# Attention and gated convolution in one kernel: near scores from 64-key steps, causal masks partly by matrix product, transforms halved instead of cut in six, weights loaded over all partitions, and a new order

## The chip, the cores and the metric

The kernel runs on one core of a Trainium2 chip. A core has five engines that run their own instruction streams side by side: TensorE (PE, matrix products into PSUM; PEld is its weight load), VectorE (DVE), ScalarE (ACT), GpSimd (POOL) and SyncE (SP), which issues the DMA transfers here. The metric is the device time of one execution in microseconds (us), lower is better; a profiled execution is taken beside the timed ones.

## The reference, cut to what matters

First attention over 4 batches, 8 heads, 768 positions and 64 values a head, then a gated long convolution on its output.

```python
scores = (1 / sqrt(64)) * q @ k.T                    # per batch and head, 768 x 768
rel = pos[:, None] - pos[None, :]
causal = rel >= 0
stream_keep = causal & ((pos[None, :] < 4) | (rel < 64))   # 4 sink keys, window of 64
mask = where(is_retrieval[head], causal, stream_keep)      # heads 0, 2, 6 are retrieval heads
a = softmax(where(mask, scores, -1e9)); attn = a @ v
x = attn as (batch, 768, 512)
x1, x2, x3 = split(x @ w_proj)                       # three times 512 columns
conv = irfft(rfft(x2) * rfft(filter))                # over the 768 positions
out = (x1 * conv * x3) @ w_out                       # float32, 4 x 768 x 512
```

## The kernel before

The heads are worked in 16 pairs `n`, four to a batch: `PAIRS = (1, 3, 0, 2)` puts head `hp` with head `hp + 4`. So pairs 0 and 1 of a batch hold two streaming ("near") heads, pair 2 one retrieval ("wide") head and one near head ("mixed"), pair 3 two wide heads.

For each pair `lq`, `lk`, `lv` load float32 rows; `cq`, `ck`, `cv` cast them to bf16; `T` and `E` turn q and k into `qkT` (head dimension on the partitions, the two heads on partitions 0 to 63 and 64 to 127), by PE and an eviction for the pairs in `BY_PE` and by a DMA transpose issued from SP for the others. `sc` writes scores, keys on the partitions and queries along the row, in tiles of two PSUM banks of 512 columns, one bank a head; `ex` evicts a tile through the exponential on ACT into `pT`; `mk` multiplies what needs it with 0/1 masks on DVE. A near pair's blocks of 128 keys x 128 queries (the list `NEAR`: the diagonal, the one beside it, and key block 0 for the sink) fill tiles of 512, 512, 512 and 384 columns a head; a wide head has 21 blocks (`WIDE`). `at` sums the products of `pT` with `v_aug` (values and a column of ones), or `v_sink` where only the four sink keys count; `rec` and `nm` divide, `tn` transposes the result into `xT`.

The convolution's transform is cut in six: `hv` adds and subtracts the halves of the positions, the four `sv` instructions (`sums`, L404 to L422) make sums and differences of thirds, `z` multiplies them with cosines and sines `G` and `Gs` (columns 256, 256 and 128, for each of two results), `ze` evicts them. Per batch, `X` multiplies by the middle part of `w_proj`, `Xe` evicts, `pa`, `pb`, `pc` multiply by the filter's spectrum `HAB`, `c` transforms back, `ce` and `cv` join the halves; `x1` and `x3` are the outer parts of the projection with `xs` and `g`, `y` the gate, `o`, `oe` and `st` the output. The filter is loaded (`lf`), folded (`fold`, `fs`), transformed (`F`) and scaled (`H`). The projection weights are loaded in halves (`lw`), each with one transfer for partitions 0 to 63 and one for 64 to 127, and cast (`cw`).

The order is written out by hand in `ORDER`: every word is one step, `@k` names one of four PSUM slots of two banks, `/v`, `/s`, `/p` the engine of an eviction or cast (DVE, ACT, POOL; L188). Each engine runs its instructions in the order of the words and waits by semaphores; SP issues all DMAs in that order too, and a DMA that waits for a buffer holds those behind it. The buffers of q and k are three deep, of v two, of `pT` two.

## Time and profile before

| | us |
|---|---|
| median of 3 runs | 213.87 (213.72 to 214.07) |
| the profiled execution, its own time | 212.19 |
| its span, first to last instruction | 210.2 |
| exponentials (ACT, L608 and L612) | 69.3 |
| masks (DVE, L617) | 29.5 |
| sums of thirds for the 16 pairs (DVE, L408 to L421) | 23.5 |
| casts and evictions by POOL (L192) | 15.4 |

Busy time by stage, from the profile's windows of 20 us:

| us from the start | PE | DVE | ACT | POOL | DMA GB/s |
|---|---|---|---|---|---|
| 0 to 20 | 15.0 | 17.0 | 17.4 | 5.1 | 272 |
| 20 to 40 | 13.9 | 19.0 | 18.5 | 6.4 | 218 |
| 40 to 60 | 17.4 | 17.1 | 16.5 | 4.6 | 232 |
| 60 to 80 | 15.4 | 15.6 | 14.8 | 2.3 | 172 |
| 80 to 100 | 17.2 | 19.5 | 16.6 | 0.0 | 196 |
| 100 to 140 | 36.4 | 35.2 | 34.5 | 1.5 | 178 |
| 140 to 180 | 38.4 | 35.6 | 25.5 | 0.8 | 106 |
| 180 to 200 | 18.9 | 15.3 | 8.4 | 0.0 | 140 |

How to read it: in the page's slices each digit is the busy share of a 40th of the span in tenths. A group's line gives the line of the code, engine, operation, tiles and shapes, count, then busy us and mean ns of one, then the engine's idle time before it. The chain is followed back from the last instruction. Matrix products are pipelined, so PE's busy time counts overlap; the distance between starts is what they cost in a row. Successive instructions of DVE and ACT overlap a little too, so that busy times of groups add up to more than the engine's (by about 0.06 us an instruction on DVE and 0.08 on ACT).

### The profile page before, as it was taken

To read this page: it belongs to the slowest core of one execution; us is meant where nothing else is said; L and a number is where in the kernel's file an instruction comes from. 1 tells how busy PE (TensorE), PEld (TensorE's weight loads), DVE (VectorE), ACT (ScalarE), POOL (GpSimd) and SP (SyncE) were. 2 spreads that over 40 slices of the span, in tenths; PEclk is the share of its full clock that TensorE was granted. 3 is DMA by queue.
4 is the path that set the end of the run, shared out by engine and by line. 5 is a ranking of instruction groups with operands and counts; after the bars stand their busy time and mean duration, and the time that the engine had idled before them with its cause. 6 is when DMAs were issued, how large, how long until landed. Compare 5 with 4: busy or idle time off the path is not lost.

```text
span 210.2 us, 4229 instructions
## 1 busy us (share of the span) xinstructions
PE 176.2 (84%) x1594; PEld 101.3 (48%) x1606; DVE 175.0 (83%) x391; ACT 154.9 (74%) x203; POOL 20.6 (10%) x38
## 2 busy tenths in 40 slices
PE   7867758689867796998879996999999799997970
PEld 2434535556423463455633664566446466454420
DVE  7898999998699929999789997899999876786810
ACT  7899988978974597997869995996896445441550
POOL 7020513231160000000000000010010000000000
PEclk9999999889996999999999999999999999999997
DMA  6999999999999564999996889919961300252462
GB/s 185 337 316 239 212 239 209 206 198 341 170 297 255 85 100 94 197 259 203 222 250 93 189 197 211 196 37 265 234 159 37 75 0 0 50 205 100 158 255 101
DMA packets 77174, 37.71 MB, mean 179 GB/s; under 512 B 65435, under 2 KB 70682, under 8 KB 77146
## 3 DMA queue, kind: packets, MB, share of 16 engines
q1 hardware_dynamic: 77146, 37.36, 79.2%
q8 instruction: 14, 0.23, 0.5%
q14 instruction: 14, 0.11, 0.2%
HBM read 24.64 MB, written 6.29 MB: 147 GB/s over the span
## 4 chain that ended last, share of the span: by engine, by line
PE 47%; DMA 15%; SPq 11%; DVE 10%; ACT 9%; issue 4%; DVEq 0%; ACTq 0%
PE x_ps L764 12%; DMA qk_f<-in_k_dram 10%; PE out_ps L816 10%; PE X_ps L727 8%; PE c_ps L789 5%; DMA filt<-in_moe_filter_fft_dram 5%; PE sc L597 4%; PE att L651 4%; PE z_ps L703 3%; SPq L539 2%; SPq L542 2%; SPq L397 2%; SPq L553 2%; ACT pT L608 2%; ACT HAB L462 2%
## 5 line engine op out<-in xcount | busy, mean ns | idle before, releaser
L608 ACT ACTIVATE pT<-sc 128x1024 bf16<-128x1024 f32 (+2 forms) x72 | 65.9, 972 | 9.3 <-PE sc L597 7.5
L764 PE MATMUL x_ps<-xT,wproj 128*128 128x384 bf16 x256 | 47.0, 327 | 3.4 <-POOL wproj L192 2.3
L764 PEld LDWEIGHTS <-wproj 128*128 128x128 bf16 x256 | 23.8, 98 | 21.2 <-POOL wproj L192 3.0
L597 PE MATMUL sc<-qkT 64*128 64x256 bf16 (+3 forms) x236 | 24.7, 293 | 9.0 <-DVE gy L779 2.8
L727 PE MATMUL X_ps<-wproj,Z 128*128 128x512 bf16 x92 | 23.2, 389 | 0.3
L789 PE MATMUL c_ps<-Gi,P 128*128 128x384 bf16 x96 | 18.7, 326 | 5.5 <-ACT evs L194 4.5
L800 DVE TENSOR_TENSOR conv<-evs,c_ps 128x384 bf16<-128x384 f32 x32 | 16.2, 551 | 7.9 <-ACT evs L194 2.9
L816 PE MATMUL out_ps<-wout,gy 128*128 128x512 bf16 x91 | 21.9, 379 | 0.4 <-issue 0.2
L651 PE MATMUL att<-v_aug,pT 128*128 128x65 bf16 x472 | 20.8, 193 | 1.0 <-ACT pT L608 0.3
L651 PEld LDWEIGHTS <-pT 128*128 128x128 bf16 x552 | 19.0, 97 | 4.6 <-issue 2.3
L597 PEld LDWEIGHTS <-qkT 64*128 64x128 bf16 x236 | 10.0, 94 | 22.0 <-issue 15.7
L194 ACT CAST x1s<-x_ps 128x768 bf16<-128x768 f32 x16 | 12.9, 808 | 8.0 <-PE x_ps L764 7.2
L617 DVE TENSOR_TENSOR pT<-pT,band 128x512 bf16<-128x512 bf16 (+4 forms) x36 | 17.1, 486 | 0.0
L194 ACT CAST Z<-z_ps 128x768 bf16<-128x768 f32 x15 | 12.1, 811 | 5.8 <-PE z_ps L703 5.8
L194 ACT COPY o<-out_ps 128x1024 f32<-128x1024 f32 (+1 forms) x14 | 12.3, 877 | 5.5 <-PE out_ps L816 5.4
L666 DVE TENSOR_TENSOR attn<-att,rec 128x768 bf16<-128x768 f32 x16 | 15.2, 953 | 0.3
L789 PEld LDWEIGHTS <-P 128*128 128x128 bf16 x96 | 8.9, 97 | 12.2 <-issue 6.9
L570 PE MATMUL qkT_ps<-identity,qk_bf 128*128 128x128 bf16 x120 | 10.7, 234 | 4.5 <-DVE qkT L190 1.5
L816 PEld LDWEIGHTS <-gy 128*128 128x128 bf16 x96 | 9.1, 98 | 10.7 <-issue 0.8
L727 PEld LDWEIGHTS <-Z 128*128 128x128 bf16 x96 | 8.9, 100 | 10.9 <-issue 2.0
L194 ACT CAST X<-X_ps 128x1024 bf16<-128x1024 f32 x11 | 11.2, 1028 | 3.6 <-PE X_ps L727 3.5
L192 POOL CAST v_sink<-v_f 4x128 bf16<-4x128 f32 x8 | 3.4, 429 | 103.9 <-DMA v_f<-in_v_dram 103.0
(107 smaller groups left out, 285.4 us busy)
## 6 DMA issues: line engine op xcount, KB each, us to landing
v_f<-in_v_dram SPq DMA_DIRECT2D x32, 192.0 KB, 5.3
out_dram<-o SPq DMA_DIRECT2D x9, 512.0 KB, 3.5
qk_f<-in_k_dram SPq DMA_DIRECT2D x10, 384.0 KB, 4.8
qk_f<-in_q_dram SPq DMA_DIRECT2D x10, 384.0 KB, 5.3
w_f<-in_moe_w_proj_dram SPq DMA_DIRECT2D x12, 256.0 KB, 7.2
qk_f<-in_q_dram SPq DMA_DIRECT2D x12, 192.0 KB, 4.4
qk_f<-in_k_dram SPq DMA_DIRECT2D x12, 192.0 KB, 4.4
filt<-in_moe_filter_fft_dram SPq DMA_DIRECT2D x2, 768.0 KB, 8.7
```

Source lines behind the costliest of these rows:

```text
L194: nc.scalar.copy(out=out, in_=in_)
L570: nc.tensor.transpose(ps[:, a, t * 128:(t + 1) * 128], qk_bf(n)[:, a, t].rearrange("p hh d -> p (hh d)"), identity())
L597: nc.tensor.matmul(sc[:, z, m * 128:(m + cnt) * 128], lhsT=qkT(n)[rows, 1, j * 128:(j + 1) * 128], rhs=qkT(n)[rows, 0, i * 128:(i + cnt) * ...
L608: nc.scalar.activation(out=p[:, :, 0:w[0]], in_=sc[:, :, 0:w[0]], func=AF.Exp, scale=SCALE)
L617: nc.vector.tensor_mul(near(), near(), which())
L651: nc.tensor.matmul(att[:, hh, 65 * i:65 * i + 65], lhsT=pT(n)[:, s, z, 128 * m:128 * m + 128], rhs=v_aug(n)[:, j, hh, :] if far or j >= i ...
L666: nc.vector.tensor_mul(attn(n).rearrange("p i hh d -> p hh i d"), rows[:, :, :, 0:64], held[f"rec.{n}"][:, :, :, None].to_broadcast([128, ...
L727: nc.tensor.matmul(ps[:, u, :], lhsT=held[f"Z.{b * HP + at}"][:, r, f, :], rhs=wproj()[:, PAIRS[at], DM:2 * DM], start=(at == 0), stop=(at ...
L764: nc.tensor.matmul(ps[:, s, 0:HS], lhsT=wproj()[:, cc, part * DM + cb * 128:part * DM + (cb + 1) * 128], rhs=xT(b)[:, cc, s * HS:s * HS + HS],
L789: nc.tensor.matmul(ps[:, r, 0:HS].rearrange("p (m t) -> p m t", m=NM), lhsT=P(b)[:, t, u, ch], rhs=Gi()[:, :, r, f, :], start=(m == 0), st ...
L800: fn(conv[:, half * HS:half * HS + HS], held[f"evs.{b}.{cb}"], held[f"c_ps.{b}.{cb}"][:, 1, 0:HS])
L816: nc.tensor.matmul(ps[:, i % 2, :], lhsT=gy(b)[:, cb, i * 128:(i + 1) * 128], rhs=wout()[:, cb, :], start=(cb == 0), stop=(cb == NC - 1))
```

## The change

- **Weights.** A load of half a projection is one transfer for each of its two 128-row parts, over all 128 partitions. For that the two heads of a pair are interleaved in `attn` (last two dimensions `d hh` in place of `hh d`), so `nm` writes every second element.
- **Near scores.** For a near head the diagonal block of 128 keys is computed, and over its unused quarter (keys 64 to 127, queries 0 to 63) the scores of the 64 keys before it: 11 products of 128 or 64 columns. The sink's scores come from `k_sink`, the four keys at columns 0 and 32 of a tile of zeros, in one product for both heads of a near pair. A near pair has tiles of 1024, 512 and 640 columns. `mo` shifts the keys-before part of `pT` with a mask into `pN`, `mk` masks what stays; `ks` and `vs` (one for each near head) fill the sink tiles.
- **Masks by TensorE.** For the pairs in `HIDDEN` the wide heads' diagonal blocks get -1e30 added by a product of `identity` with `hide`, and their `mk` goes.
- **Halved.** For pairs 0 to 7 `z` works on `hv` itself, three products of 384 columns for each result, and `sv` goes; the later pairs stay as they were.
- **Order.** `ORDER` is written anew from its first word, with new PSUM slots and engines. Words with `/p`: q casts 0 to 10, k casts 0 to 8, v casts 0 to 8, weight casts 8 to 5, sink copies 8 to 17. DVE's q and k casts go from 22 to 6, its v casts 12 to 4, its evictions of qkT 8 to 10, of Z 1 to 5, of `ce` 3 to 7, of x1 0 to 2.

```diff
 BY_PE = {0, 1, 2, 3, 4, 5, 7, 9, 11, 13}
+HIDDEN = {2, 3, 6, 7, 10, 11}
 TURNED = {0, 1, 2, 3, 4}
+HALVED = {0, 1, 2, 3, 4, 5, 6, 7}
 PAIRS = (1, 3, 0, 2)
 RETRIEVAL = (0, 2, 6)
 W = 512
...
-NEAR = [
-    [(0, 0), (0, 1), (0, 2), (0, 3)],
-    [(0, 4), (0, 5), (1, 1), (1, 2)],
-    [(2, 2), (2, 3), (3, 3), (3, 4)],
-    [(4, 4), (4, 5), (5, 5)],
-]
+MIXED = WIDE[:3] + [[(3, 3), (3, 4), (3, 5), (5, 5)], [(4, 4), (4, 5), (0, 4), (0, 5)], [(1, 5)]]
 
 ORDER = """
-ident table mblank blank1@0 mbelow mband lk0 sinT quarter tcol blank2@1 fcol lq0 tfrac angle2 angle1 turns1 wrap1
-turns2 band0 wrap2 turns0 angle0 ck0/s size1 wrap0 sin1 ones0 cos1 T0.1@2 sin0 cq0/v lq1 size0 cos0 T0.0 expT cq1/v
...
+table quarter blankN1 zero0 mover sinT lq0 lk0 tcol tfrac mblank blank0@0 lk1 lq1 lq2 mband ident blank1@1 blank3@2
+fcol angle1 angle0 turns0 angle2 turns2 turns1 wrap2 mbelow wrap1 cq0/s wrap0 size0 ck1/p ck0/v T0.1@3 size1 sin1
+ones0 E0.1/v cq1/v over sin0 cos0 band0 T1.1@0 T0.0 E0.0/v zero1 lk2 cos1 expT ks0.0/v T1.0 sc0.1@1 cq2/s band1
+ks0.1/p E1.1/v ks1.1/v below par ex0.1 parb alt ck2/p sc0.0@2 sc0.2@3 T2.1@1 ones1 ex0.0 blankN0 T2.0 lv0 lk3
...
+lk9 x30.2.0@1 nm7 tn7 H2.0.2/s z6.0@3 H2.1.2/s hv7.0 x30.2.1 z6.1 H2.2/s ze6/s lq9 ck8/s hv7.1 sw0.0 fs.3 H3.0 H3.1
+g0.2 z7.1@0 H3.2 z7.0 F1.1@3 F0.1@1 F1.0 H1.2/s ck9/p cq9/p ze7/v F0.0 H1.0/s H2.0.1/s H0.2/v H1.1/v pa0.1 H0.1/s
+x31.0.1@0 pb0.1 x31.0.0 x11.0.1@3 H0.0/s X1.2.1@2 x11.0.0 pc0.1 X1.0.1@1 X1.2.0 pa0.2 xs1.0/s T9.1@3 lq8 cq8/p T9.0
+X1.0.0 pa0.0 pb0.0 g1.0 x11.2.0@0 E9.1/s E9.0/v sc9.1@3 x11.2.1 Xe1.2/s Xe1.0/s pc0.0 ex9.1 pb0.2 x11.1.0@2 pc0.2
+Gi lk11 c0.1.0@1 xs1.2/v T8 sc9.0@3 c0.1.1 c0.3.1@0 ce0.1/v cv0.1.0 cv0.1.1 y0.1 x11.1.1 ex9.0 mo9.1 mo9.0 ks8.1/p
+xs1.1/s mk9.1 c0.3.0 ce0.3/s ks9.1/p x31.2.1@3 cv0.3.0 sc8.1@1 ks8.0/s ex8.1 sc8.0@2 x31.2.0 cv0.3.1 y0.3 ks9.0/s
+ex8.0 mo8.1 mk8.1 ck11/s sc8.2@1 c0.0.0@0 c0.0.1 lq11 c0.2.1@2 cq11/p ex8.2 lk10 c0.2.0 g1.2 pa1.0 x30.3.0@1
+ce0.0/s cv0.0.1 lq10 cv0.0.0 T11.0@3 ck10/s x30.3.1 ce0.2/s y0.0 T11.1 cq10/p g0.3 X1.1.0@0 E11.0/s X1.1.1 mo8.0
...
+o3.1.0@1 o3.1.1 oe3.1/s st3.5 st3.1 o3.0.0@0 o3.0.1 oe3.0/v st3.0 o3.2.0@2 o3.2.1 oe3.2/s st3.2
...
 def _slots(wide):
-    if wide[0] == wide[1]:
-        return [[(0, blocks), (1, blocks)] for blocks in (WIDE if wide[0] else NEAR)]
+    if all(wide):
+        return [([(0, 0, "wide", blocks), (1, 1, "wide", blocks)], (128 * len(blocks),) * 2) for blocks in WIDE]
+    if not any(wide):
+        return [([(z, z, "near", range(8)) for z in range(2)], (W, W)),
+                ([(z, z, "near", range(8, 12)) for z in range(2)], (256, 256)),
+                ([(0, None, "sink", range(1, 5)), (1, None, "sink", range(5, 6))], (W, 128))]
     far, near = (0, 1) if wide[0] else (1, 0)
-    both = [[(far, a), (near, b)] for a, b in zip(WIDE[:4], NEAR)]
-    return both + [[(far, WIDE[4]), (far, WIDE[5])]]
+    other = [(near, "near", range(8)), (near, "near", range(8, 12)), (near, "sink", range(1, 5)),
+             (near, "sink", range(5, 6)), (far, "wide", MIXED[5])]
+    return [([(0, far, "wide", MIXED[c]), (1,) + other[c]], (W, (W, 256, W, 128, 128)[c])) for c in range(5)]
...
+    @op("hide")
+    def _():
+        nc.vector.tensor_scalar(out=hide(), in0=below(), scalar1=1e30, scalar2=-1e30, op0=ALU.mult, op1=ALU.add)
...
-    def weights(part):
+    def weights(part, c):
 
         if part < 3:
-            rows = moe_w_proj[:, part * DM:part * DM + DM].rearrange("(hh c p) n -> hh p c n", hh=2, p=64)
-            return [(slice(64 * hh, 64 * hh + 64), rows[hh]) for hh in range(2)]
-        return [(slice(0, 128), moe_w_out.rearrange("(c p) n -> p c n", p=128))]
+            return moe_w_proj[:, part * DM:part * DM + DM].rearrange("(hh c d) n -> c d hh n", hh=2, d=64)[c]
+        return moe_w_out.rearrange("(c d hh) n -> c d hh n", hh=2, d=64)[c]
...
-                for at, rows in weights(part):
-                    nc.sync.dma_start(out=w[at], in_=rows[:, cs])
+                for c in range(2):
+                    nc.sync.dma_start(out=w[:, c], in_=weights(part, 2 * half + c))
...
     def attn(n):
-        return buf(f"attn.{n}", [128, NT, 2, 64], BF16, f"attn{n % 2}")
+        return buf(f"attn.{n}", [128, NT, 64, 2], BF16, f"attn{n % 2}")
...
+    def k_sink(n):
+        return buf(f"k_sink{n % 3}", [128, 128], BF16)
+
+    def pN(n):
+        return buf(f"pN{n % 2}", [128, 2, NT - 1, 128], BF16)
+
+    SINK = [slice(32 * hh, 32 * hh + n_sink) for hh in range(2)]
...
-        if n_sink and not all(wide):
-            @op(f"vs{n}")
-            def _(n=n):
-                ev(v_sink(n)[0:n_sink, :, 0:64], held[f"v_f32.{n}"][0:n_sink, :, 0])
+        for hh in range(2):
+            if not wide[hh]:
+                @op(f"vs{n}.{hh}")
+                def _(n=n, hh=hh):
+                    ev(v_sink(n)[SINK[hh], hh, 0:64], held[f"v_f32.{n}"][0:n_sink, hh, 0])
+
+                @op(f"ks{n}.{hh}")
+                def _(n=n, hh=hh):
+                    rows = slice(64 * hh, 64 * hh + 64)
+                    ev(k_sink(n)[rows, SINK[hh]], qkT(n)[rows, 1, 0:n_sink])
...
+        def products(n, z, hh, kind, which):
+            if kind == "sink":
+                rows = slice(0, 128) if hh is None else slice(64 * hh, 64 * hh + 64)
+                cols = slice(128 * which.start, 128 * which.stop)
+                return [(rows, 0, k_sink(n)[rows], qkT(n)[rows, 0, cols])]
+            rows = slice(64 * hh, 64 * hh + 64)
+            kT, qT = qkT(n)[rows, 1], qkT(n)[rows, 0]
+            if kind == "wide":
+                return [(rows, 128 * m, kT[:, j * 128:(j + 1) * 128], qT[:, i * 128:(i + cnt) * 128])
+                        for m, j, i, cnt in _runs(which)]
+            out = []
+            for u in which[::2]:
+                col, own = 64 * (u - which.start), slice(64 * u, 64 * u + 128)
+                out.append((rows, col, kT[:, own], qT[:, own]))
+                if u:
+                    out.append((rows, col, kT[:, 64 * u - 64:64 * u], qT[:, 64 * u:64 * u + 64]))
+            return out
+        for c, (parts_, w) in enumerate(slots):
             @op(f"sc{n}.{c}")
-            def _(n=n, c=c, banks_of=banks_of):
+            def _(n=n, c=c, parts_=parts_, products=products):
                 sc = banks(f"sc.{n}.{c}")
-                todo = [[(z, hh) + tuple(run) for run in _runs(blocks)] for z, (hh, blocks) in enumerate(banks_of)]
+                todo = [[(z,) + one for one in products(n, z, *rest)] for z, *rest in parts_]
+                hidden = [[(z, slice(0, 128), 128 * m, identity(), hide()) for m, (j, i) in enumerate(which) if i == j]
+                          if kind == "wide" and n in HIDDEN else [] for z, hh, kind, which in parts_]
+                todo = [some + more for some, more in zip(todo, hidden)]
                 for at in range(max(map(len, todo))):
-                    for one in todo:
-                        if at >= len(one):
-                            continue
-                        z, hh, m, j, i, cnt = one[at]
-                        rows = slice(64 * hh, 64 * hh + 64)
-                        nc.tensor.matmul(
-                            sc[:, z, m * 128:(m + cnt) * 128],
-                            lhsT=qkT(n)[rows, 1, j * 128:(j + 1) * 128],
-                            rhs=qkT(n)[rows, 0, i * 128:(i + cnt) * 128],
-                            start=True, stop=True,
-                        )
+                    for some, more in zip(todo, hidden):
+                        if at < len(some):
+                            z, rows, col, lhsT, rhs = some[at]
+                            to = slice(128 - lhsT.shape[-1], 128)
+                            nc.tensor.matmul(sc[to, z, col:col + rhs.shape[-1]], lhsT=lhsT, rhs=rhs,
+                                             start=not more or at == 0, stop=not more or at == len(some) - 1)
...
+        if n in HIDDEN and all(wide):
+            pass
...
+            zs = slice(0, 2) if not any(wide) else slice(1, 2)
+            hs = slice(0, 2) if not any(wide) else slice(1, 2) if wide[0] else slice(0, 1)
+            cnt = zs.stop - zs.start
+            for c, gs in ((0, range(0, 4)), (1, range(4, 6))):
+                late = range(max(1, gs.start), gs.stop)
+                factor(f"mo{n}.{c}",
+                       lambda n=n, c=c, zs=zs, gs=gs, late=late:
+                       pT(n)[64:128, c, zs].rearrange("p z (g w) -> p z g w", w=128)
+                       [:, :, late.start - gs.start:late.stop - gs.start, 0:64],
+                       lambda cnt=cnt, late=late:
+                       over()[64:128, None, None, :].to_broadcast([64, cnt, len(late), 64]),
+                       lambda n=n, hs=hs, late=late: pN(n)[64:128, hs, late.start - 1:late.stop - 1, 0:64])
+                factor(f"mk{n}.{c}",
+                       lambda n=n, c=c, zs=zs, gs=gs: pT(n)[:, c, zs, 0:128 * len(gs)],
+                       lambda cnt=cnt, gs=gs:
+                       (band() if gs.start == 0 else band()[:, 1:3]).rearrange("p g w -> p (g w)")[:, None, :]
+                       .to_broadcast([128, cnt, 128 * len(gs)]))
+            if any(wide) and n not in HIDDEN:
+                factor(f"mk{n}.2", lambda n=n: pT(n)[:, 0:4, 0, 0:128],
                        lambda: below()[:, None, :].to_broadcast([128, 4, 128]))
...
+                    own = v_aug(n)[:, :, hh, :]
+                    if wide[hh]:
+                        todo = [(pT(n)[:, c, zz, 128 * m:128 * m + 128], own[:, j])
+                                for j, (c, zz, m) in ((j, place[(hh, (j, i))]) for j in range(i + 1))]
+                    else:
+                        todo = [(pT(n)[:, i // 4, z, 128 * (i % 4):128 * (i % 4) + 128], own[:, i])]
+                        if i:
+                            c, zz = (2, z * any(wide)) if i < 5 else (2 + any(wide), 1)
+                            at = 128 * (i - 1) if i < 5 else 0
+                            todo += [(pN(n)[:, hh, i - 1], own[:, i - 1]),
+                                     (pT(n)[:, c, zz, at:at + 128], v_sink(n)[:, hh, :])]
+                    for at, (lhsT, rhs) in enumerate(todo):
+                        nc.tensor.matmul(att[:, hh, 65 * i:65 * i + 65], lhsT=lhsT, rhs=rhs,
+                                         start=(at == 0), stop=(at == len(todo) - 1))
...
-            nc.vector.tensor_mul(attn(n).rearrange("p i hh d -> p hh i d"), rows[:, :, :, 0:64],
+            nc.vector.tensor_mul(attn(n).rearrange("p i d hh -> p hh i d"), rows[:, :, :, 0:64],
...
+        if n not in HALVED:
+            sums(f"sv{n}", hv, tv, av)
 
         for r in range(2):
             @op(f"z{n}.{r}")
-            def _(n=n, r=r, tv=tv, av=av):
+            def _(n=n, r=r, hv=hv, tv=tv, av=av):
                 ps = banks(f"z_ps.{n}")
+                if n in HALVED:
+                    for m in range(NM):
+                        nc.tensor.matmul(ps[:, r, 0:HS], lhsT=hv()[:, r, m],
+                                         rhs=G()[:, m, r].rearrange("p t f -> p (t f)"),
+                                         start=(m == 0), stop=(m == NM - 1))
+                    return
```

## The prediction

> **What bounds the kernel now.** I read the page's busy times and slices first, then the chain that ended last (its shares, then in order of time), then the groups by shape, the timelines of POOL and VectorE around the eight weight casts, and the DMA view from 50 to 60 us.
>
> The page, with slices of 5.26 us:
>
> ```profile
> span 210.2 us, 4229 instructions
> ...
> PE 176.2 (84%) x1594; PEld 101.3 (48%) x1606; DVE 175.0 (83%) x391; ACT 154.9 (74%) x203; POOL 20.6 (10%) x38
> ...
> PE   7867758689867796998879996999999799997970
> ...
> DVE  7898999998699929999789997899999876786810
> ACT  7899988978974597997869995996896445441550
> ...
> DMA  6999999999999564999996889919961300252462
> ```
>
> The chain in order of time (start, length, what):
>
> ```profile
> 44.72 10.90 DMA filt<-in_moe_filter_fft_dram
> ...
> 134.67 0.33 PE sc L597 x4
> ...
> 168.99 5.20 PE x_ps L764 x32
> ...
> 200.13 3.63 PE out_ps L816 x16
> 203.78 0.58 ACT o L194
> ```
>
> There are two stages. Up to about 85 us (the first scores of pair 8 start at 84.7) PE has gaps, while DVE, ACT and, to 73 us, the DMA engines are full: the chain runs through loads and DVE. From 100 us on it is nearly all PE, to 203.8; 6.4 us of eviction, store and end follow.
>
> The chain prices PE: 32 products of 384 columns take 5.20 us, 0.423 ns a column. Four score products of 256 columns take 0.33 us where 4 x 256 x 0.423 would be 0.43: the two heads, on different halves of the rows, run side by side (0.22), and entering and leaving the 64-row shape costs 0.11. A 65-column attention product takes 0.0305 (60 in 1.82). All groups priced so are about 165 us of PE work: 53 before pair 8's scores, 111 behind them, done in 203.8 - 84.7 = 119 us (93.5%).
>
> The groups that the change removes or moves, and POOL's casts beside DVE (start, duration):
>
> ```profile
> L608 ACT ACTIVATE pT<-sc 128x1024 bf16<-128x1024 f32 x52 | 52.1, 1041 | 7.9 <-PE sc L597 6.7 <-issue 1.0
> L421 DVE SCALAR_TENSOR_TENSOR av<-tv,hv 128x256 bf16<-128x256 bf16 x16 | 7.4, 471 | 0.0
> L408 DVE TENSOR_TENSOR tv<-hv 128x256 bf16<-128x256 bf16 x16 | 6.0, 383 | 0.0
> L413 DVE TENSOR_TENSOR tv<-hv 128x256 bf16<-128x256 bf16 x16 | 5.3, 328 | 0.3
> ```
>
> ```profile
> 61.85 1.14 POOL L192 CAST wout<-w_f 128x1024 bf16<-128x1024 f32 x1 [0.70 <-DMA w_f<-in_moe_w_out_dram]
> 62.01 1.12 DVE L408 TENSOR_TENSOR tv<-hv 128x256 bf16<-128x256 bf16 x1
> ```
>
> Each of the eight POOL casts stretches a DVE instruction beside it: 0.33, 0.72, 0.75, 0.65, 0.27, 0.84, 0.83 and 0.83 us over its usual length, mean 0.65.
>
> DMA, 50 to 60 us, forty slices of 0.25 us: 385 is the filter, 188 to 90 from 52.5 us the last projection weights (64 partitions a transfer), 393 near 58 us the output weights (128 partitions).
>
> ```profile
> DMA  9999999999989996899992861119999979990862
> GB/s 377 385 393 385 393 385 385 393 287 188 188 156 229 229 180 131 157 207 257 150 90 78 77 39 36 18 30 285 288 292 407 393 270 393 393 393 0 49 74 74
> ```
>
> **The change part by part.** Shapes come from the diff, engines and order from the words of the new order.
>
> *Weights.* 3.1 MB at some 190 GB/s are 16.5 us of full DMA engines, at 390 they are 8.1: 8 us less in a stage where they are full to 73 us. Ends: 0 (the rate stays) and 8. SP issues 16 transfers where it issued 14, 0.6 us each, among loads that wait for buffers anyway: nothing, or 1.2 us if that cover goes. It lets loads come earlier; by itself it ends nothing, since DVE is full too.
>
> *Near scores, ACT.* A pair of two near heads has 3 x 1.041 + 0.827 = 3.95 us of exponentials; after, 1024, 512 and 640 columns: 1.04 + 0.65 + 0.74 (between the 512 and 768 rows) = 2.43. Eight pairs: -12.2. A mixed pair goes 4.79 to 4.40, four: -1.6. Evictions to other engines (Z 4 x 0.81, evs 4 x 0.48, and the like) less new copies: -8.7. With 0.08 of overlap between instructions, ACT goes from 155 to about 134.
>
> *DVE.* Sums of eight pairs: 8 x (0.471 + 0.383 + 0.328 + 0.299) = -11.8. Masks: a near pair 2.07 to 1.75 (the 1024, 512, 384 and 256 rows), mixed hidden ones 2.07 to about 1.25, wide hidden ones 1.26 to 0: -2.6 - 2.5 - 3.8. Casts of q, k, v to POOL or ACT: 16 x 0.57 + 8 x 0.55 = -13.5. Taken on: qkT 2 x 0.95, Z 4 x 0.96, evs 4 x 0.56, x1 2 x 0.95, two weight casts, an xT and an output eviction: +12.9; 13 small sink copies x 0.21: +2.7. Sum -18.6; 42 fewer instructions overlap by 0.06 less: about -16.
>
> But POOL gets 26 casts of 768 columns and keeps 5 of 8 weight casts. By the mean above, scaled by 0.75, each stops DVE for 0.49: 26 x 0.49 - 3 x 0.65 = +11. Ends: nothing (if DVE is then in instructions that read PSUM; no such instruction lies beside a cast in this trace), and the cast's whole 1.1 us (1.47, the median of the weight casts, by 0.75), +29. I take +11, as eight of eight showed it: DVE about 170, so moving these casts frees next to nothing there.
>
> The copies that shift keys' products into `pN` start at partition 64; no row shows one. Nothing beyond the 384-column row to 0.06 of lost overlap on each side, 24 x 0.12 = 2.9; I take nothing, with 2.9 in the upper end. `nm` writes every second element: its row (0.953 for 768 from PSUM) is as long as the contiguous qkT copy (0.952), so nothing; at worst 16 x 0.3.
>
> *PE.* Halved instead of sixth-size transforms: (2304 - 1280) columns x 0.423 = 0.43, eight pairs +3.5. Added masks: 54 products of 128 columns x 0.054 = +2.9. Near scores: columns side by side 1920 to 1728 (6 x 128 + 5 x 64 + 640), so about nothing in columns. But products with 64 and 128 keys now alternate, eight changes of shape a pair, which no row shows; the nearest is the 64-row block's 0.11 for in and out, 0.055 a change. Ends: 0 and 0.11. Twelve pairs with a near head: +5.3 (0 to 10.6), less eight blocks at 0.11. Attention +20 products: 0.6. Together PE goes from 165 to about 175.
>
> The Trainium skill, TensorEngine Tiling, Key Properties, says that changing the tiling mode drains the engine, and its Restrictions that column tiling loses fast weight loads. TensorE: Matmul & The Clock Gate, LDWEIGHTS, gives columns / 1.2 ns, so by an estimate from that page a 64-column load bare on the path is 53 ns, 10 a near pair and 5 a mixed one, 5.3 us on top; no run here shows it, and the sum would end 2 to 5 us later.
>
> *Order.* Everything is placed anew. Words ahead of pair 8's scores, priced as above: PE 53 becomes 73 (X of two batches and several x1 and x3 come earlier), DVE 72 becomes 70, and 76 with the stops of 21 POOL casts (11, of which 5 were in the rows before), ACT 71 becomes 68. New waits: the sink scores need `ks`, a copy of qkT, and attention needs `pN`. POOL runs in turn, so a cast that waits for its load holds the copies behind it (`ks8.1` behind `cq8`), and PE waits at the pair's last scores with what stands behind them; SP has T8 waiting for its casts ahead of later loads, as before. At the start POOL fills `pN` before the identity and `fcol`: up to 1.2 us on the sines, covered by the first loads, which land at 4.2.
>
> **The sum.** The first attention starts at 16.2 us and I leave it there. From there to pair 8 PE has 73 - 8 = 65 us of work, DVE 76 - 12 = 64. Before, DVE was busy 85% of this stretch and 4 us of its idle time was the filter chain at 73 to 79 us; at 88% for either engine it takes 73 us: pair 8 at about 89, 4 us later than before, with 20 us more PE work done. Behind it are 99 + 2.6 = 102 us of PE, at the 93.5% of before 109. End of PE 198, span 198 + 6.4 = 204.4. The profiled execution was 212.19 for a span of 210.2, and the median of the runs is 213.87: add 3.7. **Prediction: 208 us**, with a range of its own of 203.5 to 212.5 (stage one at 84 to 92%).
>
> **Rivals.**
> - *Everything overlaps better.* For it: ACT loses 21 us and DMA 8, and the late stage had 90% on DVE and 86% on ACT beside PE. At 94% in stage one (pair 8 at 85) and 96% behind, without drains (103): 194.4 + 3.7 = 198 us, reaching to 203.5.
> - *POOL stops DVE for whole casts* (the other side). 31 casts x 1.1 in place of 0.49 and 0.65: DVE 188, and 88 by pair 8. At 88% pair 8 comes at 16 + 76 / 0.88 = 102, and the end at 102 + 109 + 6.4 = 217.4, 221 us; slower than before from about 0.75 us a cast. For it: a cast took up to 2.33 us. Against: 0.84 was the longest stretch. 214.3 to 221.
> - *Changes of shape cost 0.11 or more, with loads bare.* Another 5.3 us of PE by the upper end, and twice that if the loads lie bare as well, half of it in each stage; in stage one DVE's 64 us lie beside it, so I count a third of that half: 3.5 to 8 us, 211.5 to 216, either side of before.
> - *The weights still load at 190 GB/s.* The full DMA engines then hold the fifth to seventh pair as now; pair 8 at 93, 212 us. This would make the change not what it says; against it stands the 393 row.
>
> **How the numbers follow.** Forecast 0.47, better overlap 0.17, POOL 0.16, shapes 0.12, weights 0.08. Measurements can tell 0.2% (0.43 us) from no change. Faster: 0.47 + 0.17 + half of the shapes + most of the weights = 0.75, less 0.03 for the forecast's own edge: 0.72. Same 0.04, slower 0.24. The range leaves out about a tenth on each side: 200 to 217.
>
> **What would show it.** Right: the exponentials of near pairs in three instructions, ACT near 134; 390 GB/s under the weight loads; pair 8's scores at 85 to 93 us and PE without long gaps behind them; DVE instructions stretched by about 0.5 beside POOL casts. Wrong: score blocks of near pairs over 0.9 us on PE; DVE above 180; DVE at the end of most PE waits after 100 us; a POOL queue that sc and T wait for.

## The result, and the profile after

The changed kernel takes 220.83 us (median of four runs, 220.44 to 221.89) where the kernel before takes 213.81: 1.0334 times as long, interval 1.0297 to 1.0372. The forecast was 208 us, its range 200 to 217: wrong in sign, and 12.8 us off. The profiled execution had a span of 219.8 us and a time of its own of 221.89. The runs of one kernel spread by some per cent; below, runs more than 1.5% above the fastest of their kernel are set aside as slow, and ratios, intervals and the column of kept runs leave them out.

The page of the changed kernel (slices of 5.5 us):

```profile
span 219.8 us, 4589 instructions
...
PE 195.7 (89%) x1767; PEld 114.3 (52%) x1784; DVE 175.3 (80%) x353; ACT 135.4 (62%) x186; POOL 41.8 (19%) x74
...
PE   4878996699999899899999999899999999996990
...
DVE  5799789356938999897899999879879899595940
ACT  6956661836778757765797964583699633532331
...
PEclk9999589579999999999999999999999999999997
DMA  6989795199089948999659979997195640205064
```

ScalarE is down from 154.9 to 135.4 us (134 was forecast), VectorE has stayed at 175 (170 forecast), and PE is up by 19.5 us of busy time, not by 10. PE is at 8 or 9 in nearly every slice from 44 us on. Two stretches of half clock (the granted clock was 0.50, a 5 in the row `PEclk`) stand at 22 to 29 and at 40 to 46 us.

The chain in order of time, around pair 8's scores:

```profile
97.89 1.14 PE x_ps L831 x7
99.02 0.49 PE c_ps L856 x3
99.51 0.98 PE sc L646 x14
100.49 1.08 PE c_ps L856 x6
101.57 0.65 PE x_ps L831 x4
102.22 0.49 PE c_ps L856 x3
102.71 0.65 PE x_ps L831 x4
103.36 1.60 PE sc L646 x22
```

A score block of 14 products takes 0.98 us, and a pair's two near blocks together (14 and 8 products) 1.60, as much as ten of the 384-column products of `x_ps`. The score line holds 13% of the chain, where it held 4%.

The row of the widest masks before, and then the groups of the changed kernel that answer to those shown of before:

```profile
L617 DVE TENSOR_TENSOR pT<-pT,band 128x1024 bf16<-128x1024 bf16 x8 | 5.5, 684 | 0.0
```

```profile
L653 ACT ACTIVATE pT<-sc 128x1024 bf16<-128x1024 f32 x32 | 32.3, 1025 | 12.8 <-PE sc L646 10.9 <-issue 1.7
L662 DVE TENSOR_TENSOR pT<-pT,band 128x512 bf16<-128x512 bf16 x12 | 7.4, 621 | 0.1
L662 DVE TENSOR_TENSOR pT<-pT,band 128x1024 bf16<-128x1024 bf16 x8 | 7.2, 912 | 0.1
L662 DVE TENSOR_TENSOR pN<-pT,over 64x384 bf16<-64x384 bf16 x8 | 3.8, 476 | 3.3 <-ACT pT L653 3.2
L662 DVE TENSOR_TENSOR pN<-pT,over 64x256 bf16<-64x256 bf16 x8 | 3.5, 448 | 0.5 <-ACT pT L653 0.3
```

The exponentials of near pairs are gone as foreseen, 20 fewer of 1024 columns; but ScalarE now waits 10.9 us for score blocks (6.7 before). The masks are slow: one of 1024 columns took 0.684 us before and takes 0.912 here.

Starts of a few steps on PE (us), found by matching the order of its weight loads with the written order of the work; "grouped" and "weights alone" are experiments below:

| first load or product of | before | after | grouped | weights alone |
|---|---|---|---|---|
| pair 0's attention | 16.2 | 18.3 | 16.1 | 15.5 |
| pair 3's attention | 33.9 | 43.0 | 39.7 | 33.9 |
| pair 6's attention | 73.6 | 75.1 | 70.5 | 69.1 |
| pair 8's scores | 84.7 | 103.3 | 97.9 | 80.8 |
| the last batch's products for x1 | 170.0 | 179.4 | 172.6 | 166.0 |

The new order puts pair 8's second score block ahead of its first; the first block alone starts at 103.9 and 98.3 us, the figures that the expectations below use. From pair 8's scores to the end of PE (214.4) there are 111.1 us, where 109 were forecast. Nearly the whole miss lies ahead of them: 103.3 us where 89 were forecast. 2 us of it lie ahead of the first attention, which was left at 16.2 us and came at 18.3.

### The profile page after: what moved, and what is told of

It reads as the page before. It is cut to its first block, busy times and chain, and to the rows that moved or that the text cites. A ratio compares the mean times of both kernels' runs of the same rounds, so it can differ in the third digit from the quotient of the medians.

```text
span 219.8 us, 4589 instructions
## 1 busy us (share of the span) xinstructions
PE 195.7 (89%) x1767; PEld 114.3 (52%) x1784; DVE 175.3 (80%) x353; ACT 135.4 (62%) x186; POOL 41.8 (19%) x74
## 4 chain that ended last, share of the span: by engine, by line
PE 53%; DVE 31%; ACT 8%; issue 5%; POOL 0%; DVEq 0%; ACTq 0%; POOLq 0%
PE sc L646 13%; PE x_ps L831 9%; PE X_ps L794 7%; PE att L715 6%; PE c_ps L856 5%; DVE pT L662 5%; PE out_ps L883 4%; PE blank_ps L239 3%; DVE gy L846 3%; ACT pT L653 3%; DVE qkT L194 3%; DVE attn L726 2%; PE qkT_ps L600 2%; DVE halves L445 2%; DVE conv L867 2%
## 5 line engine op out<-in xcount | busy, mean ns | idle before, releaser
L653 ACT ACTIVATE pT<-sc 128x1024 bf16<-128x1024 f32 (+2 forms) x48 | 41.9, 901 | 17.2 <-PE sc L646 15.3
L646 PE MATMUL sc<-qkT 64*128 64x128 bf16 (+4 forms) x316 | 36.1, 254 | 3.2 <-ACT qkT L198 1.8
L646 PEld LDWEIGHTS <-qkT 64*128 64x128 bf16 (+1 forms) x316 | 17.5, 98 | 20.6 <-issue 10.7
L715 PEld LDWEIGHTS <-pT 128*128 128x128 bf16 x472 | 21.2, 102 | 6.3 <-DVE pT L662 3.6
L196 POOL CAST qk_bf<-qk_f 128x768 bf16<-128x768 f32 x18 | 16.0, 896 | 31.2 <-DMA qk_f<-in_k_dram 20.2
L198 ACT CAST x1s<-x_ps 128x768 bf16<-128x768 f32 x14 | 11.1, 798 | 13.9 <-PE x_ps L831 9.0
L198 ACT COPY o<-out_ps 128x1024 f32<-128x1024 f32 (+1 forms) x13 | 11.4, 881 | 10.9 <-PE out_ps L883 10.8
L657 ACT ACTIVATE pT<-sc 128x640 bf16<-128x640 f32 (+1 forms) x20 | 14.1, 723 | 5.2 <-PE sc L646 3.4
L662 DVE TENSOR_TENSOR pT<-pT,band 128x512 bf16<-128x512 bf16 (+2 forms) x24 | 16.5, 689 | 0.4
L883 PEld LDWEIGHTS <-gy 128*128 128x128 bf16 x96 | 8.8, 98 | 10.2 <-DVE gy L849 0.7
L662 DVE TENSOR_TENSOR pN<-pT,over 64x384 bf16<-64x384 bf16 (+3 forms) x24 | 10.3, 439 | 4.2 <-ACT pT L653 3.5
L198 ACT COPY qkT<-qkT_ps 128x768 bf16<-128x768 bf16 x10 | 7.9, 801 | 9.0 <-DVE qkT L194 4.6
```

Of the source, the lines that this page charges most:

```text
L196: nc.gpsimd.tensor_copy(out=out, in_=in_)
L198: nc.scalar.copy(out=out, in_=in_)
L646: nc.tensor.matmul(sc[to, z, col:col + rhs.shape[-1]], lhsT=lhsT, rhs=rhs, start=not more or at == 0, stop=not more or at == len(some) - 1)
L653: nc.scalar.activation(out=p[:, :, 0:w[0]], in_=sc[:, :, 0:w[0]], func=AF.Exp, scale=SCALE)
L662: nc.vector.tensor_mul((to or near)(), near(), which())
L715: nc.tensor.matmul(att[:, hh, 65 * i:65 * i + 65], lhsT=lhsT, rhs=rhs, start=(at == 0), stop=(at == len(todo) - 1))
```

## The experiments

Ratios are to the kernel before, run on the same chip beside each (medians of 211.5 to 212.8 us there), with a 95% interval; where there is none, too few runs were left. From chip to chip the kernel before itself had medians from 211.5 to 213.8 us, so where a difference is given by the ratios and by the medians, the first is the safer.

| kernel | median us, all runs | of the runs kept (how many) | ratio to before |
|---|---|---|---|
| changed kernel, scores grouped by shape | 214.12 | 214.12 (10 of 10) | 1.0124 (1.0072 to 1.0175) |
| no 64-key shape at all | 213.09 | 212.36 (8 of 10) | 1.0005 (0.9956 to 1.0054) |
| grouped, gaps of PE taken away | 213.31 | 213.31 (4 of 4) | 1.0105 (0.9997 to 1.0212) |
| the same without added masks | 217.54 | 217.54 (4 of 4) | 1.0225 (1.0118 to 1.0333) |
| changed kernel, key copy moved | 220.84 | 218.38 (2 of 4) | 1.0326 (1.0186 to 1.0465) |
| changed kernel, filters loaded earlier | 218.77 | 217.06 (2 of 4) | |
| changed kernel, casts on VectorE | 233.26 | 233.26 (4 of 4) | 1.1009 (1.0875 to 1.1143) |
| all of the change, order of before | 227.59 | 225.57 (2 of 4) | |
| weights and near scores, order of before | 224.33 | 224.33 (4 of 4) | 1.0559 (1.0451 to 1.0667) |
| the same, grouped | 215.49 | 213.88 (2 of 4) | 1.0102 (0.9976 to 1.0229) |
| the same, no 64-key shape | 214.46 | 213.85 (8 of 10) | 1.0068 (1.0013 to 1.0122) |
| that, without the sinks' key copies | 214.15 | 210.31 (1 of 4) | |
| that, without the copies into pN | 210.93 | 209.04 (4 of 10) | 0.9972 (0.9915 to 1.0030) |
| that, without both | 208.11 | 207.61 (3 of 4) | 0.9865 (0.9746 to 0.9984) |
| weights alone | 208.50 | 208.50 (4 of 4) | 0.9862 (0.9762 to 0.9961) |
| weights, halved transforms | 206.46 | 206.40 (3 of 4) | 0.9743 (0.9632 to 0.9855) |
| weights, added masks | 208.04 | 208.04 (4 of 4) | 0.9835 (0.9746 to 0.9923) |
| weights, halved transforms, added masks | 210.95 | 210.18 (8 of 10) | 0.9906 (0.9853 to 0.9959) |

### What a change of shape costs

The changed kernel issues, for each 128 queries, a product of 128 keys and one of 64, the two heads in turn. The first edit sorts each block by shape:

```diff
-                out.append((rows, col, kT[:, own], qT[:, own]))
+                owns.append((rows, col, kT[:, own], qT[:, own]))
                 if u:
-                    out.append((rows, col, kT[:, 64 * u - 64:64 * u], qT[:, 64 * u:64 * u + 64]))
-            return out
+                    steps.append((rows, col, kT[:, 64 * u - 64:64 * u], qT[:, 64 * u:64 * u + 64]))
+            return owns + steps
...
+                for at, some, more in sorted(turn, key=lambda one: shape(*one[1][one[0]][1:4])):
```

> The changed kernel with one edit: inside a score block all products of 128 keys come first, then all of 64 keys, then the added masks. By the groups of the two profiles the eight near pairs lose 6 of their 8 changes of shape each, and the mixed pairs about as many. Theory S (a change of shape costs about 0.125 us and PE bounds both stages): the first score block of a near pair falls from 1.0 to about 0.55 us, the second from 0.67 to about 0.42; PE's busy time falls by 7 to 9 us, pair 8's scores come at 99 to 101 instead of 103.9 us and the time falls to 212 to 215 us. Theory O (stage one is held by the new order: waits along the chain and the held queue of SP): PE's work falls as much, but pair 8's scores stay at 102 to 104, and only the half of the saving that lies behind them shows: 216 to 218 us. If the changes cost the 0.055 us of the prediction: 218 to 220 us.

The second takes the 64-key shape away:

```diff
-                    out.append((rows, col, kT[:, 64 * u - 64:64 * u], qT[:, 64 * u:64 * u + 64]))
+                    out.append((rows, col, kT[:, own], qT[:, 64 * u:64 * u + 64]))
```

> The changed kernel with each 64-key product replaced by one with 128 keys and the same columns, so that a near block has no change of shape inside; it takes the wrong keys there, so part of the near scores is not computed. Theory S (a change of shape costs 0.11 us, by the grouped blocks): the first near block falls from 0.98 to about 0.35 us and the second from 0.62 to about 0.2, PE's work falls by about 11 us against the changed kernel, and the time, by the 0.84 of the grouped kernel, by 9: 210 to 213 us. If what is left after the grouping is not shapes but copies and waits: no faster than the grouped kernel, 213.5 to 215 us.

The chain of the grouped kernel, and then that of the one with a single shape, at a pair's two near blocks:

```profile
131.37 0.94 PE sc L648 x22
```

```profile
137.78 0.59 PE sc L645 x22
```

The same 22 products: 1.60, 0.94, 0.59 us, with nine changes of shape, three and none. That is 0.11 us a change for the first six and 0.12 for the last three. (The kernel with a single shape multiplies by the wrong keys in the 64-key products, so its near scores are partly left out.) The Trainium skill, TensorEngine Tiling (Array Packing), Key Properties, says that changing the tiling mode drains the engine and gives no price; here it was 0.11 to 0.12 us. PE's busy time fell by 8.0 us by grouping (195.7 to 187.7) and the time by 4.5 us by the ratios (1.0334 to 1.0124), 6.7 by the medians; with one shape alone PE's busy time fell by 10.2 us and the time by 7.0 and 7.7. So theory S holds for the difference to the kernel before: without the changes of shape the changed kernel is as fast as before (1.0005). It does not explain why it is not faster, as forecast.

### Half clock, gaps and loads

```diff
-... E4.0/v sc3.3@2 E4.1/s ex3.3 cw1.0/v ...
+... E4.0/v sc3.3@2 ex3.3 E4.1/s cw1.0/v ...
```

> The changed kernel with one edit: pair 4's first key copy on ScalarE goes behind the exponential that PE's next bank waits for. The gap of PE at 37.3 to 40.2 us should close to under 1 us. Theory B (gap, then half clock): the second stretch of half clock (39.5 to 46.4 us) goes too, pair 4's attention comes 5 to 6 us earlier, and the time is 215 to 218 us. If only the wait itself counts, at most 3 us earlier there and 218 to 220 us; if VectorE's chain ends the stage anyway, 220 to 222 us.

The edit missed its aim. PE's timeline in the changed kernel, and then with the edit:

```profile
40.18 0.80 PE L734 MATMUL xt_ps<-identity,attn 128*128 128x128 bf16 x6 [2.88 <-ACT pT L653]
```

```profile
40.81 0.49 PE L599 MATMUL qkT_ps<-identity,qk_bf 128*128 128x128 bf16 x6 [2.29 <-DVE qkT L193]
```

The transposes of pair 2 no longer wait for ScalarE, but the next ones wait for a copy that stands in VectorE's queue behind a normalisation, two sums and a cast. The gap stayed, and so did the time (1.0326 beside 1.0334). In the grouped kernel the same edit was made together with four products of zeros (`blank4@0`) ahead of `sc2.1@0`:

> The regrouped kernel with two edits that take PE's gaps in stage one away: four products of zeros are put ahead of pair 2's first scores (a gap of 1.0 us there), and the first key copy of pair 4 on ScalarE goes behind the exponential that frees the bank PE waits for (a gap of 3.0 us at 34 to 37 us). Theory B (the gaps make the clock halve for the next 3.4 or 6.8 us, and that is lost on a stage that PE bounds): no half clock between 15 and 60 us, pair 3's attention at 35 to 36 us instead of 39.8, pair 8's scores at 92 to 94 instead of 98.3, and 208 to 211 us. If the stage is bound by chains of waits through VectorE and ScalarE and not by PE's rate: pair 3's attention gains up to 3 us but it is lost again by pair 8's scores, 213 to 214.5 us.

The clock rows of the grouped kernel and of this one:

```profile
PEclk9999599699999999999999999999999999999999
```

```profile
PEclk9999999799999999999999999999999999999997
```

The first stretch of half clock is gone, and pair 3's attention came at 35.6 us as theory B said (39.7 in the grouped kernel), but pair 8's scores only at 94.4 (97.9), and the times can't be told apart (1.0105 and 1.0124). What the clock is worth is seen better from all runs. Taking, for each of 88 executions of sixteen of these kernels (all but the three without the copies), the span and the clock time lost (span times one minus the mean granted clock), each against its own kernel's mean, a microsecond of clock lost goes with 0.57 us of span (correlation 0.80). In the two profiled executions the changed kernel lost 6.8 us to half clock ahead of its end, the kernel before 3.4: by this some 2 us of the difference, an estimate. Other kernels here differ more: the mean loss of a run is 7.7 us in the changed kernel, 6.6 grouped, 4.5 with the gaps taken away, 7.5 without the added masks as well, 13.4 with the casts on VectorE, and in the order of before 16.7 with the near scores and 7.4 with them grouped. Part of their differences goes with the clock, then; whether lost clock is the cause or follows from the waits, no run separates.

```diff
-... lf1 ex6.1 ... mo6.1 lf0 ...
+... lv4 cq6/p lf1 lf0 T6 ...
```

> The changed kernel with one edit: both filter loads are issued ahead of pair 6's transpose on SP, some 20 us earlier. Theory L (the late filter, held behind weight loads that wait for their buffers, delays stage one): the halves fold at 55 to 60 us instead of 71 to 76, pair 8's scores come 3 to 6 us earlier, 215 to 218 us. Theory S, or any in which PE's own work bounds stage one: DMA idles elsewhere, the time stays at 220 to 222 us.

218.77 us, with runs of 216.09, 218.02, 219.52 and 220.63, two of them inside theory L's range. But the edit missed its aim: the filter's halves fold at 68.4 us instead of 71.4, not at 55 to 60, since the fold has its place in VectorE's order. In the changed kernel it stands there without any wait for the filter (the last number of its row is VectorE's idle time before it), so the late filter held nothing up there:

```profile
L445 DVE TENSOR_TENSOR halves<-filt,filt 128x1536 bf16<-128x1536 f32 x2 | 4.3, 2165 | 0.0
```

Pair 3's attention, ahead of anything that the filters touch, was already 3.3 us earlier in its profile, since the first stretch of half clock was not there; pair 8's scores were 3.7 earlier. By this profile theory L falls. The runs' spans follow the clock: 214.0 us at a mean of 0.986, 218.6 at 0.964.

### The parts in the order of before

To part the arithmetic from the placement, the changed functions ran with the words of the kernel before's order: a fourth score block dropped, new copies beside the words they depend on.

```diff
-E1.1/v ones1 lv0 ex0.2 band2 vs0/p T2.0@3 sc0.3@0 E2.0/v mk0.2 T2.1 lq4 ex0.0 ...
+E1.1/v ks1.0/p ks1.1/p ones1 lv0 below hide blankN1 ex0.2 vs0.0/p vs0.1/p T2.0@3 E2.0/v mo0.1 T2.1 lq4 ex0.0 ...
```

> All of the change (weights over all partitions, near scores in three blocks, halved transforms for eight pairs, added masks), but in the order of the kernel before: its words stay where they were, the fourth score block of a near pair and the words that are no longer needed are dropped, the copies to the sinks follow the copies of qkT, and each second copy into pN stands beside its mask. The casts of q, k and v stay on VectorE and ScalarE as before. Theory O (the new placement costs the time): 206 to 212 us, pair 8's scores at 85 to 92 us. Theory S (the arithmetic itself costs it): 217 to 222 us, with the near score blocks at 1.0 and 0.65 us as in the changed kernel.

227.59 us (runs from 224.65 to 228.81), slower than either theory said: the parts cost the time also without the new order, which is some 5 to 7 us better for them than the old one. Theory O falls.

Then the same with `HALVED` and `HIDDEN` empty, and the words of the sums and masks back in their places:

> As the one before (all of the change in the kernel before's order), but without halved transforms and without added masks: the sums and causal masks stay on VectorE. It leaves PE some 6.4 us less work (3.5 for the transforms, 2.9 for the masks, by the prediction's rows) and VectorE 18 us more. If PE bounds both stages (theory S), it is 4 to 6 us faster than the full change in the same order. If VectorE still bounds stage one, as in the kernel before, it is 3 to 8 us slower than the full change in the same order.

224.33 us, 1 to 3 less than the full change, with runs that overlap. VectorE has 14 us more to do in it (175.0 against 160.9) and it is not slower, so VectorE alone does not bound this stage; whether PE's 6.4 us count is not shown.

From the other side, the kernel before with single parts added:

```diff
-            rows = moe_w_proj[:, part * DM:part * DM + DM].rearrange("(hh c p) n -> hh p c n", hh=2, p=64)
-            return [(slice(64 * hh, 64 * hh + 64), rows[hh]) for hh in range(2)]
+            return moe_w_proj[:, part * DM:part * DM + DM].rearrange("(hh c d) n -> c d hh n", hh=2, d=64)[c]
...
-        return buf(f"attn.{n}", [128, NT, 2, 64], BF16, f"attn{n % 2}")
+        return buf(f"attn.{n}", [128, NT, 64, 2], BF16, f"attn{n % 2}")
```

> The kernel before with the weights part alone: projection weights loaded over all 128 partitions in contiguous rows of two, and the interleaved attention layout that goes with it; the order stays. The prediction put its own worth at 0 to 8 us of DMA, and nothing at the end by itself since VectorE is full as well: 211 to 213.5 us beside a kernel before of 212.8. If the loads hold stage one, as its chain through loads says: 206 to 210 us. If writing every second element in the normalisation is slow (0.3 us each, 16 of them): 214 to 217 us.

208.50 us, a ratio of 0.9862: 4 us at the median and near 3 by the ratio, from a part that was given nothing by itself. Pair 3's attention comes at 33.9 us in both profiles, pair 6's 4.5 us earlier, and the DMA engines and SP's queue hold 14% of the chain instead of 26%: this points at the loads.

```diff
-        sums(f"sv{n}", hv, tv, av)
+        if n not in HALVED:
+            sums(f"sv{n}", hv, tv, av)
```

> The kernel before with the weights part (208.5 us) and halved transforms for the first eight pairs, whose 32 words for the sums are dropped from its order. VectorE is spared 11.8 us and PE gets 3.5 us. If VectorE bounds stage one there: 204 to 207.5 us. Theory E (PE bounds stage one, so that work moved to it shows): 209 to 212 us. If neither is bound by its own work but by the chain of loads: 207.5 to 209 us.

206.46 us, 0.9743, the fastest of all kernels here, as expected if VectorE bounds the first stage; the interval still overlaps that of the weights alone. VectorE is at 166.4 us, and PE holds 55% of the chain.

```diff
+                for z, more in enumerate(hidden):
+                    for m in more:
+                        nc.tensor.matmul(sc[:, z, m * 128:(m + 1) * 128], lhsT=identity(), rhs=hide(),
+                                         start=False, stop=m == more[-1])
```

> The kernel before with the weights part (208.5 us) and the added causal masks of six pairs, whose 15 words for the masks on VectorE are dropped. VectorE is spared about 6.2 us (3.8 for the wide pairs and 2.5 for the mixed) and PE gets 2.9 us by its rows, and up to 2 us more for entering the 128-row shape in a score block. If VectorE bounds stage one: 205 to 208 us. Theory E (PE bounds): 209 to 213 us.

208.04 us: no difference to the weights alone that the intervals tell.

> Both together, so everything of the change but the near scores and the new order. VectorE is spared 18 us, PE gets 6.4 us. If VectorE bounds stage one: 201 to 206 us, and then the near scores and the order alone are what costs time in the changed kernel. Theory E (PE bounds): 211 to 215 us.

210.95 us: together they do not add up. The first expectation misses by some 5 us, and the time lies at the fast edge of theory E's range. VectorE is down to 161.9 us and PE's share of the chain is up to 65% (55% and 49% with one of them): it looks as if PE bounds once VectorE has been freed so far, which was not tried further.

> The kernel before with the weights part and the near scores alone, with all products of 128 keys ahead of those of 64 keys in each block (so few changes of shape), in the kernel before's order with the copies into the sinks and into pN added. If only the changes of shape made the near scores slow: 204 to 209 us, no slower than the weights part alone (208.5). Theory N (their copies, one behind another from the transposed keys to the sink scores and from the exponentials to the attention, cost time too): 212 to 218 us. The same without the grouping took 224.3 us.

215.49 us against 224.33 interleaved: 9 to 10 us less with the grouping, of which some 5 go with the clock by the estimate above (7.4 us lost instead of 16.7). But the weights alone are at 208.50, so the near scores cost 5 us by the ratios and 7 by the medians, though ScalarE has 11 us less to do (143.1 against 154.4).

### What is left of the near scores

> The weights part and the near scores in the kernel before's order, with the 64-key products replaced by 128-key ones (wrong keys, so part of the near scores is not computed). Grouped it took 215.5 us, interleaved 224.3, and without the near scores 208.5. Theory S (the rest is shapes too): 209 to 212 us. Theory N (the copies into sinks and pN and the waits on them cost the rest): 213 to 217 us.

214.46 us, 1.0068 (1.0013 to 1.0122): theory N. With no change of shape inside the blocks PE is at 174.4 us, as with the weights alone (174.9), and still 4 us are lost by the ratios, 6 by the medians. So the additions were taken away one by one:

```diff
-                return [(rows, 0, k_sink(n)[rows], qkT(n)[rows, 0, cols])]
+                return [(rows, 0, qkT(n)[rows, 1, 0:128], qkT(n)[rows, 0, cols])]
```

> As the kernel before (weights part, near scores with 128-key products, the kernel before's order, 214.5 us), without the copies of the sink's keys and their zero fills: the sink scores take the first 128 keys as they lie, so they are not the sink's alone (part of the scores is wrong). If the copy and PE's wait for it (POOL's queue, then the pair's last scores) are what remains: 209 to 212 us. If not: 213.5 to 215 us.

Runs of 210.31, 213.97, 214.32 and 216.10 us: one inside the range for the sink copies, the others not. What the sink copies cost by themselves stays open.

```diff
-                factor(f"mo{n}.{c}",
-                       ...
-                       lambda n=n, hs=hs, late=late: pN(n)[64:128, hs, late.start - 1:late.stop - 1, 0:64])
```

> As the kernel of 214.5 us, without the 24 copies that shift a pair's half masks into pN (pN stays zero, so the keys of the window ahead are left out of the attention). VectorE is spared 24 x about 0.3 = 7 us. If those copies, which attention waits for, are what remains: 209 to 212 us. If not: 213.5 to 215 us.

210.93 us, 0.9972 (0.9915 to 1.0030); the kernel leaves the keys of the window ahead out of the attention. In its profile pair 8's scores start at 81.0 us, against 86.1 with the copies and 80.8 with the weights alone. The rows of the copies in the kernel of 214.46:

```profile
L663 DVE TENSOR_TENSOR pN<-pT,over 64x384 bf16<-64x384 bf16 x8 | 2.9, 360 | 0.2
L663 DVE TENSOR_TENSOR pN<-pT,over 64x256 bf16<-64x256 bf16 x8 | 2.3, 289 | 0.2
L663 DVE TENSOR_TENSOR pN<-pT,over 64x192 bf16<-64x192 bf16 x4 | 1.0, 256 | 0.1
L663 DVE TENSOR_TENSOR pN<-pT,over 64x128 bf16<-64x128 bf16 x4 | 0.9, 223 | 0.1
```

7.1 us of work, each as cheap as a full-width mask of its columns, but every one stands between an exponential and the attention products. Without them 2 us (by the ratios) to 3.5 us (by the medians, on two chips) are gained.

> Without both. If the two copies together make up the cost of the near scores: 206 to 209.5 us, as the weights part alone (208.5) or below it, since ScalarE has 12 us less. If the near scores cost time for another reason (fewer and longer blocks to overlap, 15 more attention products a near head): 211.5 to 215 us.

208.11 us, 0.9865 (0.9746 to 0.9984): as the weights alone (0.9862), and clear of the kernel with both copies (1.0068). The two copies together make up what the near scores cost beside the changes of shape, as far as these intervals tell; how it divides between them they don't tell. And even then the 12 us that ScalarE was spared (142.4 against 154.4) bring nothing that can be seen.

### VectorE's side

```diff
-... ck2/p ... cq3/p ... cv1/p ...
+... ck2/v ... cq3/v ... cv1/v ...
```

> The changed kernel with the 26 casts of q, k and v that it gives to POOL on VectorE instead. By the prediction's rows VectorE takes on 26 x 0.57 = 15 us and is spared 26 x 0.49 = 13 us of stretching, 5 of them in stage one's last rows: 219 to 224 us. If POOL's casts stop VectorE for their whole length (the rival, theory C), VectorE is spared 29 us for 15: 211 to 217 us. If VectorE is not what stage one waits for, and POOL's casts were free on it: 222 to 230 us, by the extra work in VectorE's turn.

233.26 us, slower than every expectation. The mask rows and the casts of this kernel:

```profile
L725 DVE TENSOR_TENSOR attn<-att,rec 128x768 bf16<-128x768 f32 x16 | 16.3, 1016 | 0.5
L193 DVE CAST qk_bf<-qk_f 128x768 bf16<-128x768 f32 x24 | 13.1, 552 | 2.1 <-DMA qk_f<-in_q_dram 1.9
L193 DVE CAST v_aug<-v_f 128x768 bf16<-128x768 f32 x12 | 7.5, 626 | 3.8 <-DMA v_f<-in_v_dram 3.7
L661 DVE TENSOR_TENSOR pT<-pT,band 128x1024 bf16<-128x1024 bf16 x8 | 5.4, 688 | 0.1
L661 DVE TENSOR_TENSOR pT<-pT,band 128x512 bf16<-128x512 bf16 x12 | 5.0, 420 | 0.1
```

The masks are back at 0.688 and 0.420 us, so POOL's casts had stretched them. VectorE took on 26 casts, 14.7 us by its rows, but its busy time rose by 3.9 only (175.3 to 179.2): POOL's casts had cost it 10.8 us, 0.41 each, where 0.49 was forecast. (Adding up the lengths of its other instructions, which leaves the overlap between them out, gives 9.6 us, 0.37 each.) Theory C, 1.1 us each, falls. But the time rose by 12.4 us by the medians, 14 by the ratios. On VectorE a cast stands in order ahead of masks and evictions that others wait for, and it waits for loads (5.6 us in the rows above); and some 3 us of it go with the clock by the estimate above.

> The grouped kernel with the filled gap and the moved key copy (213.3 us), without the added masks: the causal masks of the six pairs are multiplied on VectorE behind their exponentials, as in the kernel before. PE is spared 2.9 us of products and some 30 changes between the 64- and 128-row shapes, VectorE takes on about 6 us. Theory E (PE bounds the new order's stage one): 209 to 212 us. If VectorE does: 214 to 218 us.

217.54 against 213.31 us. VectorE's busy time is up by 5.0 (178.3 against 173.3), PE's down by 1.3, and the time is up by 4.2 by the medians, 2.5 by the ratios; some 1.7 of that go with the clock by the estimate above. Theory E falls: in the new order too, freeing PE alone gained nothing.

## Why the prediction was wrong

*The step that failed* is "at 88% for either engine it takes 73 us: pair 8 at about 89". It sets 65 us of PE beside 64 us of VectorE as if each hid the other. The stretch took 87 us. By the profiles' windows PE was busy for 78.0 of the 87 us from 16 to 103 us, and VectorE for 68.5; in the kernel before, from 16 to 85 us, for 52.8 and 60.1 of 69. So PE took on 25 us where 20 were counted, and VectorE 8 where 4 were. With these 5 us more, 70 for PE in place of 65, the rule of 88% would have put pair 8 at 96 us, an estimate; it came at 103.3. So about half of the miss there is in the sums, and the other half in the rule itself. The runs speak for both being on the path, in turn: 8.0 us off PE's busy time gave 4.5 to 6.7 (grouping), 5.0 us onto VectorE's cost 2.5 to 4.2 (added masks undone), and 26 casts that cost VectorE 3.9 us net cost the whole 12 to 14, the clock's share of each included. The chain of the changed kernel, by engine, and that of the grouped one:

```profile
PE 53%; DVE 31%; ACT 8%; issue 5%; POOL 0%; DVEq 0%; ACTq 0%; POOLq 0%
```

```profile
DVE 42%; PE 39%; ACT 8%; issue 5%; DMA 4%; SPq 0%; POOL 0%; DVEq 0%; ACTq 0%; POOLq 0%
```

The page of before could have said so: in that stage VectorE stood mostly at 8 or 9 and PE at 6 to 8, and 20 us more of PE's work were placed in it for 4 us.

*Shapes: the mechanism was right, the size was off.* 0.055 us a change was taken, between ends of 0 and 0.11; it measured 0.11 to 0.12, and a pair's two near blocks, with the step from one to the other, hold nine changes. PE's busy time rose 10.2 us by them, where the sum had 5.3, and the time 7.0 to 7.7. The rival that put this at 211.5 to 216 us named the right mechanism and stopped at a third of its cost in stage one, since "DVE's 64 us lie beside it": the same mistake again. The sign that the prediction named, score blocks of near pairs over 0.9 us, is there.

*The pN copies*: "I take nothing". Their durations were in the mask sum and, without POOL beside them, right (1.75 us a near pair was forecast; 0.688, 0.420, 0.355 and 0.288 without POOL's casts make 1.75). Nothing was charged for what waits on them: 2 to 3.5 us in the order of before; in the new order no run shows it.

*Weights*: "by itself it ends nothing, since DVE is full too". The loads landed in 4.0 us instead of 7.2, faster as foreseen, and by themselves they end 3 to 4 us. The same rule, that a full engine hides a full queue, erred here in the other direction. `nm`, which writes every second element and was given nothing, went from 0.953 to 1.013 us, 1 us for all 16.

*POOL*: 0.49 a cast, 0.37 to 0.41 measured; the rival with whole casts fell by its own test, though its 221 us was the time measured. Moving the casts "frees next to nothing there": by busy time that was nearly right, by the whole time it was worth 12 us.

*ScalarE* at 134 (135.4), and 109 us behind pair 8's scores (111.1): near. That ScalarE is spared 21 us was given a rival of its own; the 12 us of it that the copies' experiment tried brought nothing that can be seen.

*Clock*: PE was taken at full clock but for what the stretches of before already held. 6.8 us were lost instead of 3.4, by the estimate above 2 us.

Together shapes beyond their price (7.0 to 7.7 less 5.3, some 2 us), the copies (2 to 3.5, if they cost the same in the new order) and the clock (2, an estimate) make 6 to 8 of the 12.8 us. The rest is put down here to what "either engine" left out; no run prices it by itself, and its cause stays open.

## What to carry to other kernels

When two engines have equal sums in a stage, don't let one hide the other: look whether the chain alternates between them, and if it does, charge work on either; here half of its length or more showed in the time. Count how often small products change the shape of TensorE's tiles and sort them by shape inside a block; here that alone was worth 4.5 to 6.7 us. Try the parts of a bundled change one by one: of these, the weights and the halved transforms were worth 2.6% together in the untouched order, and the near scores, as issued, cost more than that.
